# Attention and gated FFN on one core: which head pairs score with unsplit float32 q and k, where the last outputs are staged, and a rewritten order

## The chip, the cores and the metric

One core of one Trainium2 chip runs the whole program in one launch. The metric is device time in microseconds (us). The engines are named as in the profile: PE (TensorE, matmuls), PEld (its weight loads), DVE (VectorE), ACT (ScalarE), POOL (GpSimd) and SP, which here only issues DMAs.

## The reference

```python
# attention: B=8 batches, H=8 heads, S=576, D=64, float32
q_rot, k_rot = rotate(q), rotate(k)          # rotary embedding, halves of 32
scores = matmul(q_rot, k_rot.T) / sqrt(64)
attn = exp(scores - max(scores)); attn /= sum(attn) + 1e-9
x = concat_heads(attn @ v)                   # (8, 576, 512)
# gated FFN
gate = sigmoid(causal depthwise conv of x, 5 taps)
out = (gate * (x @ w_val)) @ w_out           # w_val, w_out: 512 x 512
```

The weights and the conv taps arrive as 64-bit numbers, whose two 32-bit words the kernel turns into float32 itself (`decode`, line 677).

## The kernel before

The 64 heads are worked in 32 pairs (`p`, line 786): the two heads of a pair sit in partitions 0 to 63 and 64 to 127. Four pairs make one batch, whose FFN follows. For one pair the jobs are these:

- **Load and rotate.** q and k arrive (`load`, L300, L304), each with a copy whose halves are swapped. DVE or POOL multiply both by the table (`rope_mul`, L312) and add them (`rope_add`, L318). Pair 0 alone takes another way: its swap and sum are matmuls on PE (`rope_mm`, L327) in plain float32, 288 columns at a time.
- **Split or not.** A pair in `WHOLE` (pairs 4 to 11) keeps its rotated q and k as float32: `rope_add` writes them where the matmul reads them. Every other pair is split: `qk_hi` (L342 to L346, on ACT, DVE or POOL) rounds to the shorter type float32r, and `qk_lo` (L352 for q on DVE, L355 for k on DVE or POOL) writes the remainder.
- **Scores.** There are four blocks of 128 rows of q by 576 columns of k (`s_mm`, L392) and a fifth that both heads share (`s_mix`, L402). A block of one head is two matmuls of 288 columns in an unsplit pair, and six in a split one (high x high, high x low, low x high). A float32 matmul is two records in the trace, a float32r one is one, so an unsplit pair has 32 records on L392 and a split one 48. From pair `APART` = 4 on, one job makes a block for both heads, their matmuls taking turns between the upper and the lower half of PE's rows; pairs 0 to 3 make the block of one head after the other.
- **Softmax.** DVE copies the scores out of PSUM and takes the row maximum (`s_max`, L428), ACT takes the exponential and its sum (`s_exp`, L436): nine of each per pair.
- **Transposes and values.** PE transposes the result (L412), ACT or DVE copy it back (`t_copy`, L505, L507), PE multiplies by v (L518, L528), and DVE scales (L577).
- **Gate and FFN.** Five taps (L603 to L611), a tanh (L616), a split of x (L584 to L591), then for every batch 2 x 4 accumulators of 288-column matmuls (`f_mm`, L636) with split operands. Their results go out through `o_out` (L671 on ACT, L672 on DVE) into one of two staging tiles `outs`, and by `o_dma` (L675) on SP's queue to memory. The last batch makes its accumulators of 256 and 320 columns (L898).

The eight 128-row pieces of the two weight matrices are decoded in nine steps each beside pairs 0 to 5 (`weight_step`: L688 to L690 the first, L703 the rounding).

The order of all of this is written out: `ORDER` (line 37) lists some 3,100 jobs by number, each with the engine that takes it where there is a choice (V is DVE, A is ACT, G is POOL) and with its buffer slots. `Plan.run` issues them just so, and every engine works its own instructions in that order. `FILLS` puts groups of transposes without use on PE at two steps (L443): 20 ahead of pair 0 and 5 before pair 1. PSUM has four slots for score, transpose and FFN tiles alike. `kin` has two buffers, `qin` one.

Of the kernel before, what the change touches and what calls it, by code (L numbers as in the profile page):

```python
# [33 lines left out]
APART = 4  # L34
LIFT = 0
WHOLE = range(4, 12)
ORDER = """
7 24 8 11 17 0:0 35 10 30V 113 12V 31V 13V 32:0 25V 9 14:1 1 26V 33 18V 104 19V 140 36V 15 20:2 2 3 16 27:3 37V 4 21 34 38:1 28 22 5 23A 29 114V 51:0
115 42:2 116 6 45:3 52:00 119G 147 105G 43:11 53 60:0 106 39 48:2 46:2 44 41 142G 40 47 377:100 61:23 54:3 216 49:0 153 141G 57:1 55:1 50 58:32 56
66:0 143V 59 149V 144A 76:2 148V 82A:0 74:3 62 67<149 150V 77A:0 63:1 68:0 145G 151A 72:2 64:1 75A:0 152 292 146A 107 65 223 163:0 117 378A 154:1 218V  # L40
73A 217V 160:3 69 155:02 120G 157:2 161:3 156 78:1 164:11 70 166:3 219G 79A 71 158:0 85:0 80 165 83 172:1 293G 87V:0 167:22 162 88:0 175:2 173:1 86A
294G 159 169:3 176:33 81A 186:1 225V 84A 178:2 110A 89 224V 92:0 174 177 226V 93 194A:1 108 227A 118 90 168 228 91 170:0 299 220G 94 111V 171 179<177
379 187A:1 221V 184:3 229 180:1 121G 488 190:1 185A:1 95 242:2 181 109 131 230:3 243:03 222A 182 191A 195:0 295G 192 183 231:12 188:2 96A:0 197 236:1
189A 300V 248:3 301V 244 239:2 237:0 193A 302G 232 249:1 245:1 296A 240:23 233:3 112G 303A 246:32 251:2 199A:1 304 241 200:1 204:1 238 380 493 234:3
98A:0 202 132G 381 250 205 490V 235 201 382 203 247 252:0 297G 196V 264:3 253 198V 489V 254:2 265A:0 556 260:0 122 133 97V:1 298A 262:3 270A:0 261A
# [24 lines left out]
1010:3 1003:0 791A 1016:0 1009 908V 760:1 761 1208V 904A:3 762 1011<908 1019A:0 1210V 763 1004 1012:2 966:2 1204A 1211V 968 1274V 1002 969 1026V:0  # L70
1013 1205G 1212 1017A:0 967 1344 759 970 1279 1014 1058:30 1052G 1015 1273G 971 764<1211 1059:11 765 792G 766 1061:20 1027:2 767 909V 1029 1062 793:3
1024 768 974A:2 794 795 1346G 1028V 1060 796 1025V 1063:01 975V 1030A 1206A 1031A:0 797<1030 769A 1032:0 1066:3 1022:2 910G 1057 798 1064:2 1023A 799
800 1020:1 1067 801 1033 972G:4 1073:02 1021A 1280G 1084:3 1076:00 1034:1 1085A:1 1281V 1036 1077 1074:31 1282G 1035 976V 1075 1065 1037 802V 1038
770V 1078:2 781G 1039 1068:30 1094A:1 1040A:0 1275G 824:1 1042A:3 1071:3 1079<1094 825 1069:0 803G 1283A 834:0 826 1080:1 1070 835 977V 836 1276A 837
1284 827 1090:3 1277V 1351 1086:2 1091A:1 1043V 838<1277 839 1044G 1087A 840 828<1043 1072 841 1214:32 1081 842V:1 829 973G:3 1215:12 843 830 831 1416
1217:20 1219:03 1213 1082 832A:0 905V:1 804:2 1216 1220:3 1088:1 1353G 1218 805 1083 1222:1 1097:0 806 1089A 807 978V 1092 1223 1095 1229:31 1352G
1098V 1096V 1278A 1221 808<1098 1093V 809 1232:02 911 810 811 1099A:1 1230:30 1224:10 1100:1 812A:1 1345V 1240:3 1227:1 1234:2 1241A:0 1225:3 1242:0
1354V 1101 1286:13 1243A:0 1045V 1235<1354 1231 1104:0 1355V 1233 813 1287:10 1102 1250A:0 1347V 1226 1103 1046V 1228 1356 1105 979 1348V 1423 1288
1106 1236:2 1349G 1246:1 1289:23 1237 1107 1291:23 1417G 1247A 1572 833 1244:0 1292:1 1290 814:1 1238 1041G:0 815 1239 1245A 1294:0 1248:2 1251 816
1418V 1252A 817 1293 1253 1296:30 1110G:1 1255V:0 1295 1256:0 818<1255 1425G 1297:02 1249A 819 820 1108A:1 1299:33 821 1306:3 1254V 1350G 1109V:4  # L80
822A:1 1301:02 1257 1298 1322V:1 1424G 1312:1 1302:1 1307<1322 1313A:1 1304:0 1258:0 1426G 1308:2 1300 1363:21 1111V 1047 1314:3 1427A 1260 1112V 1303
1428 1309 1259 1113V 1305 1579 1261 1366:13 1315A:1 1310 1114G 1262 1364:21 1138:1 1285 1263 1139 1358:32 1264A:2 1419G 1140 1361:2 1316:0 1141 1359:0
1362 1116:2 1574V 1117 1266A:0 1118 1317V 1581G 1119 1420A 1142<1266 1367 1143 1573V 1144 1365 1323:3 1145 1311 1320 1421V 1127:0 1321A 1128 1146 1644
# [146 lines left out]
def attn_gated_ffn(ctx: ExitStack, tc: tile.TileContext, q2, k2, v2, tab, w_val, conv_w, w_out, out, collect=None):  # L230
# [443 lines left out]
    def o_dma(b, oc, lo, hi):  # L674
        SP.dma_start(out=out[b, oc * 128:(oc + 1) * 128, lo:hi], in_=ffn[b, "o", oc, lo])  # L675
# [312 lines left out]
```

## Time and profile before

| | us |
|---|---|
| median of three runs | 632.68 |
| lowest run | 631.52 |
| highest run | 1190.62 |
| the profiled execution's own time | 632.25 |
| its span, first to last instruction | 630.5 |

The profiled execution is 0.43 us under the median, and 1.75 us of it lie outside its span. The mean granted TensorE clock was 0.996 of full speed. In the profile a busy PE is one whose modelled matmuls overlap without a gap; it can be busy and still advance slowly.

### The profile page before, as it was taken

Reading aid. Unit: us, or ns where it says so; the run is one execution under the profiler, and the core shown is the slowest. Engines: PE = TensorE matmul, PEld = TensorE weight load, DVE = VectorE, ACT = ScalarE, POOL = GpSimd, SP = SyncE. Lnnn points to the kernel's source line nnn. Section 1 sums busy time; section 2 is a strip of 40 time slices with the busy share of each in tenths; the row PEclk is TensorE's granted clock in tenths of the full one; section 3 lists DMA queues with packets and bytes.
Section 4 is the critical chain, followed back from the end, with each engine's and each line's share of the span. In section 5 each row is a group of like instructions: output and inputs, shape, how many; then the busy total and the mean of one; then the engine's idle time right before and its main releaser. Section 6 shows DMA issues by size and latency. Waiting matters only on the chain.

```text
span 630.5 us, 21237 instructions
## 1 busy us (share of the span) xinstructions
PE 621.6 (99%) x8782; PEld 523.5 (83%) x8782; DVE 541.3 (86%) x1120; ACT 466.1 (74%) x976; POOL 324.2 (51%) x296
## 2 busy tenths in 40 slices
PE   8999999999999999999999999999999999999997
PEld 7878669777797888969888889788888889889696
DVE  6999999998898898989989899889987889786571
ACT  3999998987777797688788749777787665768502
POOL 2545354454547636656665665663456765640320
PEclk9899999999999999999999999999999999999999
DMA  7546535233543233335343244234243243121102
GB/s 226 182 149 193 163 114 163 82 119 114 154 135 117 91 108 131 99 96 152 117 150 124 61 121 148 90 121 123 93 138 98 80 144 108 59 62 39 60 21 76
DMA packets 42723, 72.85 MB, mean 116 GB/s; under 512 B 15450, under 2 KB 18051, under 8 KB 42627
## 3 DMA queue, kind: packets, MB, share of 16 engines
q1 hardware_dynamic: 42082, 70.91, 36.2%
q8 instruction: 69, 1.13, 0.8%
q10 hardware_dynamic: 544, 0.59, 0.3%
q14 instruction: 28, 0.22, 0.1%
HBM read 61.89 MB, written 9.59 MB: 113 GB/s over the span
## 4 chain that ended last, share of the span: by engine, by line
PE 91%; DVE 4%; ACT 3%; issue 1%; ACTq 0%; POOL 0%; DVEq 0%; POOLq 0%
PE ps_f L636 32%; PE ps_a L518 19%; PE ps_s L392 17%; PE ps_t L412 12%; PE ps_s L402 5%; PE ps_a L528 3%; ACT p L436 2%; DVE p L428 1%; PE ps_f L443 1%; PE ps_s L412 1%; DVE qin L312 1%; ACT pt L505 1%; DVE q L352 0%; PE ps_r L327 0%; ACT o L671 0%
## 5 line engine op out<-in xcount | busy, mean ns | idle before, releaser
L436 ACT ACTIVATE p<-p,nm 128x576 f32<-128x576 f32 x256 | 197.1, 772 | 43.3 <-DVE p L428 43.0
L428 DVE TENSOR_SCALAR_CACHE_REDUCE p<-ps_s 128x576 f32<-128x576 f32 x256 | 185.0, 751 | 32.4 <-PE ps_s L392 24.9
L505 ACT COPY pt<-ps_t 128x1024 f32<-128x1024 f32 (+1 forms) x137 | 128.0, 942 | 43.1 <-PE ps_t L412 41.5
L392 PE MATMUL ps_s<-k,q 64*128 64x288 f32 x1408 | 146.8, 321 | 0.7 <-DVE p L428 0.4
L518 PE MATMUL ps_a<-pt,v 128*64 128x320 f32 (+1 forms) x1024 | 132.1, 409 | 0.2
L392 PEld LDWEIGHTS ps_s<-k,q 64*128 64x128 f32 x1408 | 116.3, 185 | 17.0 <-issue 4.1
L636 PE MATMUL ps_f<-y,wout_hi 64*128 64x288 f32 (+2 forms) x1024 | 111.2, 302 | 0.7 <-ACT o L671 0.6
L518 PEld LDWEIGHTS ps_a<-pt,v 128*64 128x64 f32 x1024 | 70.2, 137 | 48.8 <-issue 2.2
L412 PEld LDWEIGHTS ps_t<-ident,p 64*128 64x128 f32 x2172 | 90.2, 139 | 11.6 <-DVE p L428 2.8
L412 PE MATMUL ps_t<-ident,p 64*128 64x64 f32 x2172 | 96.6, 225 | 0.7 <-ACT pt L505 0.6
L606 DVE SCALAR_TENSOR_TENSOR g<-x,cw,g 128x576 f32<-128x576 f32 (+2 forms) x108 | 92.7, 866 | 1.9 <-POOL g L610 1.4
L636 PEld LDWEIGHTS ps_f<-y,wout_hi 64*128 64x128 f32 x1024 | 85.5, 186 | 2.5 <-ACT o L671 1.2
L636 PE MATMUL ps_f<-xh,wval_hi 64*128 64x288 f32 (+2 forms) x512 | 85.3, 316 | 0.0
L636 PE MATMUL ps_f<-y,wout_lo 64*128 64x288 f32 (+2 forms) x512 | 79.7, 292 | 0.0
L636 PE MATMUL ps_f<-xl,wval_hi 64*128 64x288 f32 (+2 forms) x512 | 79.1, 292 | 0.0
L636 PE MATMUL ps_f<-xh,wval_lo 64*128 64x288 f32 (+2 forms) x512 | 79.1, 292 | 0.0
L312 POOL TENSOR_TENSOR kin<-kin,tab 128x576 f32<-128x576 f32 x38 | 54.0, 1424 | 32.5 <-DVE g L606 19.5
L636 PEld LDWEIGHTS ps_f<-xh,wval_hi 64*128 64x128 f32 x512 | 51.7, 186 | 2.0 <-DVE p L428 1.0
L636 PEld LDWEIGHTS ps_f<-y,wout_lo 64*128 64x128 f32 x512 | 52.5, 185 | 0.0
L636 PEld LDWEIGHTS ps_f<-xl,wval_hi 64*128 64x128 f32 x512 | 51.6, 185 | 0.6 <-POOL xl L591 0.2
L636 PEld LDWEIGHTS ps_f<-xh,wval_lo 64*128 64x128 f32 x512 | 51.5, 184 | 0.0
L436 ACT ACTIVATION_READ_ACCUMULATOR p<-p,nm 128x1 f32 x256 | 48.6, 190 | 0.0
(132 smaller groups left out, 945.6 us busy)
## 6 DMA issues: line engine op xcount, KB each, us to landing
kin<-in_k SPq DMA_DIRECT2D x31, 576.0 KB
qin<-in_q SPq DMA_DIRECT2D x31, 512.0 KB
v<-in_v SPq DMA_DIRECT2D x32, 320.0 KB
out_t<-o SPq DMA_DIRECT2D x28, 288.0 KB
rb<-rd SPq DMA_DIRECT2D x31, 144.0 KB
rb<-rd SPq DMA_DIRECT2D x31, 128.0 KB
wst<-in_w_val SPq DMA_DIRECT2D x4, 512.0 KB
o<-in_w_out SPq DMA_DIRECT2D x4, 512.0 KB
```

The source lines that it names most:

```text
L312: return eng.tensor_tensor(out=t[:, i, a:b], in0=t[:, 0 if p < RAW else i, a:b], in1=table[:, i, a:b], op=ALU.mult)
L392: T.matmul(out=tiles[h][:, half, 0:288], lhsT=operand(p, "q", h, x, c * 128, c * 128 + 128), rhs=operand(p, "k", h, y, k0 + half * 288, k0 ...
L402: inst = T.matmul(out=st["s8"][:, half], lhsT=operand(p, "q", h, x, 512, 640), rhs=operand(p, "k", h, y, D + half * 288, D + half * 288 + ...
L412: T.transpose(out=bank[0:src.shape[1], x, k * D:(k + 1) * D], in_=src[rows], identity=ident[rows, rows])
L428: return V.tensor_scalar(out=to, in0=st[f"s{i}"], scalar1=-SCALE if p in WHOLE else -1.0, scalar2=None, op0=ALU.mult, op1=ALU.min, accum_o ...
L436: return A.activation(out=to, in_=to if lifted else st[f"s{i}"], func=AF.Exp, bias=st[f"nm{i}"], scale=-1.0 if lifted else 1.0, accum_out= ...
L443: T.transpose(out=bank[:, 0, 0:128], in_=ident, identity=ident)
L505: return A.copy(out=dst, in_=src)
L518: T.matmul(out=st[f"a{g}"][HEAD[h], 0:n], lhsT=st["v"][:, j, h, :], rhs=st[f"pt{g}"][:, h * 4 + j], start=(j == 0), stop=False)
L528: T.matmul(out=st[f"a{x}"][HEAD[h], 0:n], lhsT=st["v"][rows, 4, h, :], rhs=st["ptr"][rows, h, 0:n], start=False, stop=True)
L606: return eng.scalar_tensor_tensor(out=g, in0=x_sb, scalar=w, in1=g, op0=ALU.mult, op1=ALU.add)
L636: inst = T.matmul(out=acc[:, x, 0:hi - lo], lhsT=wt[w][HEAD[h], kc, dc * 128:(dc + 1) * 128], rhs=mv[HEAD[h], lo:hi], start=(turn == 0 and ...
```

## The change

- `WHOLE` becomes pairs 0 to 6: seven unsplit pairs in place of eight. Pairs 0 to 3 lose their rounding and remainder steps, pairs 4 to 6 stay as they are, pairs 7 to 11 gain those steps.
- `APART` becomes 1: only pair 0 makes its blocks one head at a time.
- The five transposes without use before pair 1 go.
- In the last batch, six of the eight pieces of output are staged in the halves of `kin0`, `kin1` and `qin0`, which are free by then, and one of their DMAs is issued on ACT's queue.
- `ORDER` is a new list (3,087 jobs in place of 3,096), with other choices of engine.

```diff
-APART = 4
+APART = 1
-WHOLE = range(4, 12)
+WHOLE = range(0, 7)
...
-FILLS = {13: (20, 0), 102: (5, 0)}
+FILLS = {13: (20, 0)}
...
+    def spare(b, oc, lo):
+        i = oc + 4 * (lo > 0) - 2
+        return ("kin0", "kin1", "qin0")[i // 2] + f"#{i % 2}" if b == NB - 1 and i >= 0 else None
+
     def o_out(b, two, oc, lo, hi, eng):
-        o = ffn[b, "o", oc, lo] = outs[:, plan.slots.pop(0), 0:hi - lo]
+        t = spare(b, oc, lo)
+        t = ins[t[0]][int(t[3])][:, int(t[5])] if t else outs[:, plan.slots.pop(0)]
+        o = ffn[b, "o", oc, lo] = t[:, 0:hi - lo]
...
     def o_dma(b, oc, lo, hi):
-        SP.dma_start(out=out[b, oc * 128:(oc + 1) * 128, lo:hi], in_=ffn[b, "o", oc, lo])
+        (A if b == NB - 1 and oc == 3 and lo else SP).dma_start(out=out[b, oc * 128:(oc + 1) * 128, lo:hi], in_=ffn[b, "o", oc, lo])
...
-                        add("VA", o_out, b, two, dc, x, y, r=acc, w=f"oo/{b}.{at}".replace("#", "."))
-                        add("S", o_dma, b, dc, x, y, r=f"oo/{b}.{at}".replace("#", "."))
+                        to = spare(b, dc, x)
+                        to = toks(to + ".@", R3 if to[0] == "q" else R2) if to else f"oo/{b}.{at}".replace("#", ".")
+                        add("VA", o_out, b, two, dc, x, y, r=acc, w=to)
+                        add("S", o_dma, b, dc, x, y, r=to)
```

What this makes of the order is shown at three places. The first is PE from pair 0's scores (L392, L402) to pair 1's, the transposes of pair 0 (L412) between them. Before:

```order
L392 MATMUL ps_s<-k_155,q_147 128x288 x42
L412 MATMUL ps_s<-ident,p 128x64 x4
L402 MATMUL ps_s<-k_155,q_147 128x288 x6
L412 MATMUL ps_t<-ident,p 128x64 x32
L402 MATMUL ps_s<-k_155,q_147 128x288 x6
L392 MATMUL ps_s<-k_155,q_147 128x288 x6
L412 MATMUL ps_t<-ident,p 128x64 x16
L443 MATMUL ps_f<-ident 128x128 x5
L392 MATMUL ps_s<-k_283,q_343 128x288 x24
```

Now:

```order
L392 MATMUL ps_s<-k_156,q_164 128x288 x16
L412 MATMUL ps_t<-ident,p 128x64 x16
L412 MATMUL ps_s<-ident,p 128x64 x4
L402 MATMUL ps_s<-k_156,q_164 128x288 x2
L412 MATMUL ps_t<-ident,p 128x64 x16
L402 MATMUL ps_s<-k_156,q_164 128x288 x2
L412 MATMUL ps_t<-ident,p 128x64 x16
L392 MATMUL ps_s<-k_239,q_296 128x288 x4
L412 MATMUL ps_t<-ident,p 128x64 x16
```

Pair 0's 48 float32r score matmuls on L392 have become 16 float32 ones without a break, and pair 1 starts with one block for both heads, without the five transposes ahead of it.

The second place is ACT over the exponentials of pair 0 (L436) and what stands between them: copies of transposes (L505), the rounding of pair 1's q and k (L346, L363), and steps of the weight decode (`wst`, `l`, `wval_hi`; L688 and L703 before, L694 and L709 now). Before:

```order
L436 ACTIVATE p,sums_85<-p,nm 128x576
L346 ACTIVATE q_147<-ps_r 128x256
L436 ACTIVATE p,sums_85<-p,nm 128x576 x5
L346 ACTIVATE k_283<-kin_70 128x576
L505 COPY pr<-ps_s 128x2x2x64
L436 ACTIVATE p,sums_85<-p,nm 128x576
L505 COPY pt_330<-ps_t 128x2x8x64
L346 ACTIVATE q_343<-qin_71 128x640
L505 COPY pt_364<-ps_t 128x2x8x64
L363 CAST k_283<-k_283 128x2x64
L436 ACTIVATE p,sums_85<-p,nm 128x576
L688 ACTIVATE l<-o 128x512
```

Now:

```order
L694 ACTIVATE wst<-wst 128x512
L436 ACTIVATE p,sums_85<-p,nm 128x576
L709 CAST wval_hi<-wst 128x512
L436 ACTIVATE p,sums_85<-p,nm 128x576 x5
L505 COPY pt_268<-ps_t 128x2x8x64
L436 ACTIVATE p,sums_85<-p,nm 128x576
L505 COPY pt_292<-ps_t 128x2x8x64
L436 ACTIVATE p,sums_85<-p,nm 128x576
L505 COPY pt_292<-ps_t 128x2x8x64
L436 ACTIVATE pm,sums_85<-pm,nm 128x576
```

The two roundings and the cast of pair 1 are gone from ACT, and two steps of the weight decode have come in. Ahead of the first FFN matmul ACT has 5 `qk_hi` jobs in place of 10 and 11 weight steps in place of 7; DVE has no `qk_lo` there in place of 9.

The third place is the end of ACT's list: the results of the last batch (L671 before, L677 now). Before:

```order
L616 ACTIVATE g<-g 128x576
L616 ACTIVATE g<-g 128x256
L661 CAST y_11196<-g 128x256
L671 ACTIVATE o<-ps_f 128x256
L616 ACTIVATE g<-g 128x320
L671 ACTIVATE o<-ps_f 128x256 x3
L671 ACTIVATE o<-ps_f 128x320 x4
```

Now, with the end of DVE's list behind it (L678):

```order
L677 ACTIVATE o<-ps_f 128x576
L616 ACTIVATE g<-g 128x256
L661 CAST y_11265<-g 128x320
L677 ACTIVATE o<-ps_f 128x256
L677 ACTIVATE kin_69<-ps_f 128x256 x2
L681 DMA out_t<-qin_71 128x320
L677 ACTIVATE kin_70<-ps_f 128x320
```

```order
L660 CAST y_11265<-g 128x320
L664 TENSOR_TENSOR y_11276<-g,y_11265 128x320 x2
L678 TENSOR_SCALAR o<-ps_f 128x256
L678 TENSOR_SCALAR qin_71<-ps_f 128x320 x2
L678 TENSOR_SCALAR kin_70<-ps_f 128x320
```

Before, ACT took all eight pieces; now DVE takes four of them, and the last two pieces lie one on each engine.

## Rows read from the trace of the kernel before

**Rows 1.** The page: busy us, share of the span, instructions, by engine.
```profile
PE 621.6 (99%) x8782; PEld 523.5 (83%) x8782; DVE 541.3 (86%) x1120; ACT 466.1 (74%) x976; POOL 324.2 (51%) x296
```

**Rows 2.** The page: the chain that ended last, by engine.
```profile
PE 91%; DVE 4%; ACT 3%; issue 1%; ACTq 0%; POOL 0%; DVEq 0%; POOLq 0%
```

**Rows 3.** Stretches, L392 alone: start:end, length, busy (x instructions) by engine, clock, DMA.
```profile
11.00:68.00 57.00, 26.09 (x194) 22.86 (x194) 0.97 0.56 181
68.00:212.00 144.00, 38.09 (x256) 24.16 (x256) 1.00 0.39 120
212.00:584.00 372.00, 82.61 (x960) 69.24 (x960) 1.00 0.35 109
```

**Rows 4.** The same stretches, L402 alone.
```profile
11.00:68.00 57.00, 5.99 (x48) 4.24 (x48) 0.97 0.56 181
68.00:212.00 144.00, 11.20 (x64) 5.16 (x64) 1.00 0.39 120
212.00:584.00 372.00, 25.78 (x240) 18.67 (x240) 1.00 0.35 109
```

**Rows 5.** First stretch, L443 alone.
```profile
11.00:68.00 57.00, 0.77 (x5) 0.53 (x5) 0.97 0.56 181
```

**Rows 6.** Timeline of PE: start, us, instructions [idle before, releaser].
```profile
8.01 0.65 PE L327 MATMUL ps_r<-kin,swap 128*128 128x288 f32 x2
8.50 0.65 PE L327 MATMUL ps_r<-kin,ident 128*128 128x288 f32 x2
...
17.62 0.48 PE L412 MATMUL ps_s<-ident,p 64*128 64x64 f32 x4 [1.09 <-ACT p L436]
```

**Rows 7.** Stretches of 2 us, all engines; PEclk stands behind the engines.
```profile
16.00:18.00 2.00, 0.91 (x13) 0.68 (x9) 2.00 (x7) 1.30 (x3) 1.18 (x1) 0.86 1.03 407
18.00:20.00 2.00, 2.00 (x32) 1.99 (x32) 1.73 (x5) 2.00 (x7) 0.00 (x0) 0.50 0.88 355
20.00:22.00 2.00, 2.00 (x33) 2.00 (x31) 1.93 (x3) 2.00 (x4) 0.47 (x1) 0.78 0.07 24
```

**Rows 8.** Stretches: DVE alone in two, then PE alone in the second.
```profile
24.00:93.70 69.70, 68.57 (x154) 1.00 0.50 157
93.70:216.00 122.30, 109.10 (x213) 1.00 0.39 116
...
93.70:216.00 122.30, 122.30 (x1670) 1.00 0.39 116
```

**Rows 9.** Stretches, ACT: all of it, then L688 alone.
```profile
24.00:93.70 69.70, 66.35 (x143) 1.00 0.50 157
...
0.00:94.00 94.00, 2.73 (x4) 0.98 0.54 172
```

**Rows 10.** Stretch, L346 alone (ACT).
```profile
0.00:68.00 68.00, 5.31 (x10) 0.97 0.59 190
```

**Rows 11.** Timeline of ACT: first and last of the five L346 of pair 0.
```profile
7.73 0.38 ACT L346 ACTIVATE q<-ps_r 128x256 fp32r<-128x256 f32 x1 [0.93 <-PE ps_r L327]
...
14.10 0.36 ACT L346 ACTIVATE q<-ps_r 128x256 fp32r<-128x256 f32 x1
```

**Rows 12.** Stretches, L352 alone (DVE).
```profile
0.00:68.00 68.00, 3.61 (x6) 0.97 0.59 190
...
212.00:630.00 418.00, 15.56 (x19) 1.00 0.33 102
```

**Rows 13.** Stretches, L355 alone (DVE, then POOL).
```profile
0.00:68.00 68.00, 1.65 (x3) 2.85 (x2) 0.97 0.59 190
...
212.00:630.00 418.00, 7.59 (x9) 14.25 (x10) 1.00 0.33 102
```

**Rows 14.** The chain in order of time: start, us, what.
```profile
48.49 3.04 ACT p L436 x8
```

**Rows 15.** Timeline of the last microseconds: PE, then ACT.
```profile
624.52 0.56 PE L636 MATMUL ps_f<-y,wout_hi 64*128 64x320 f32 x4 [0.58 <-ACT o L671]
...
626.64 0.77 ACT L671 ACTIVATE o<-ps_f 128x320 f32<-128x320 f32 x2 [2.17 <-PE ps_f L636]
```

More of the change, by code (lines that the diff above doesn't have):

```diff
@@ new lines @@
+575A 399 578A:1 572A 611:3 579:1 400 614 631:1 373V 620:02 667A 673V 632A:0 401<667 269V 402 580 612 621:21 403 821G 404 623:32 270 625:1 820V 615:02
+641A:0 405 395A 374G 626<641 384A 618:0 633:3 624 668G 627:3 357:014 581:2 674A 616:2 582 622 675 583 619 334V 826 628 584 335V 617 396V 585 891
+634A:0 336V 677:10 676 586 358A 629 669G 635:3 521A:4 385G 678:01 637:2 636A 680:10 408:1 409 359 638A 682:03 337V 679 410 630 827G 683:3 411 681
+639:2 685:2 642 644 684 828V 692:03 645A 646A:0 829V 643A 412<684 647:0 338 413 693:21 414 640A 822G 415 686 695:30 687:20 406A 416 893G 697:3 823A
@@ new lines @@
+1061 1205:12 1275 1267A 803<1337 1342 1073 1206:02 961G 804 817A:0 805 1208:10 806 1079:1 807V:1 1210:02 1080A 1074 1336G 808 1081:3 1211:1 1083:1
+1082A 1088 1086 1213:3 1268G 779:0 780 1031V 1089A 1090A:1 781 1087A 782 1209 1407 1220:23 1204 1084V 1269A 1027G:1 1214 1091:1 783<1269 1338G 1221:20
+784 1207 785 1223:33 786 1212 1215:12 1343G 787V:1 1233:3 1216:2 1225:0 1344G 1234A:0 1218:1 1231:1 1217 1277:23 1232V:0 1092 1345G 1222 1226<1217
+1095:1 1227:2 1339G 1280:00 818 1093 1228 1346G 1408V 962 1096 1224 1347 1094 1219 1028V:1 1414 1097 1241A:0 1278:12 1229 1237:3 1032G 1230 1098
@@ new lines @@
+1595:20 1166 1640G 1167 1593:31 1168 1605:2 1169V:0 1400G:2 1460 1779 1171:0 1606A:0 1710V 1172 1173 1596 1174 1587:32 1716V 1641A 1462A:1 1581 1463:1
+1175<1462 1459V 1715G 1176 1588:3 1594 1455 1177 1590:0 1456A 1178 1461A 1603:3 1717V 1179A:1 1597:2 1402V 1604A:0 1180 1649:10 1330V 1464 1613A:0
+1609:3 1591 1650:02 1331G 1598<1613 1262 1652:11 1465:1 1718A 1599:0 1466 1589 1780V 1467 1651 1711V 1610A 1403V 1468 1719 1600 1469 1781V 1786
+1654:02 1601 1470 1712G 1611:3 1602 1614 1655:3 1181:1 1170 1616 1182 1404V 1617A 1183 1612A 1473V:4 1151:0 1653 1657:2 1184 1782G 1152 1615A 1474V
@@ new lines @@
+2369 2526G 2409:32 2403:01 2370 2410 2456G 2413:3 2406:0 2419:2 2429A:1 2404:3 2531G 1925:1 2679 2420A:1 2414<2429 2421:0 2415:2 2457A 2223:2 2407
+2224 2533V 1926 2416 2373V:2 1927 2422A:1 1928 2374V 2225 2226 2527V 2412 2470:30 2148V 2405 1929<2527 2471:00 1930 2534A 2417 2227<2405 2680G 2473:12
+2472 1931 1932 2535 2465:30 1933A:0 2228 2681V 1934 2229 2464 2468:1 2230 2375G 2423:1 2392 2466:3 2425:0 2231 2234:3 2426A 2235 2418 2424V 2432:2
+2528G 2236 2474 2237 2430 2427 2078 2480:01 2751 2433V 2371A:4 2220V 2238<2433 2434A:1 2469 2239 2481:20 2435:1 2221G 2240 2686 2467 2483:32 2241
@@ new lines @@
+2895 2276 2757V 2585 2704:32 2833G 2277:3 2705 2586 2764 2713:1 2587A:1 2443G:0 2708:02 2729V:0 2589A:3 2448V 2714<2729 2278 2707 2711:1 2279 2588G:1
+2280 2715:3 2712 2719:2 2709:2 2297:1 2444G:0 2716 2298 2720V:0 2299 2710 2727:0 2300 2717 2723:2 2515G:2 2718 2590V 2281<2709 2724A 2732 2282 2825V
+2283 2284 2516V:3 2730 2301<2590 2285A:1 2734V:0 2725:2 2449G 2731V 2735:0 2591V 2733A 2628:3 2692 2728A 2629 2726A:0 2302 2303 2304 2721:0 2736
+2305V:0 2834G 2617:2 2722A 2630 2592V 2631 2618 2835 2619 2770:10 2593V 2902 2620 2594 2826G 2773:20 2632<2593 2633 2771:31 2634 2286 2635 2896G
@@ L160 @@
+3068 3085V 3069 3084 3070 3086 3071V 3073A 3074 3072
 """
[L161 removed]
+FILLS = {13: (20, 0)}
 class Plan:
```

223 lines of the change are left out of this document (101 added, 122 removed).

## The prediction

> **What bounds the kernel now.** I read the page first: PE is busy for 621.6 us of 630.5 [rows 1], and the chain that ended last lies on PE for 91% of the span [rows 2]. So what the change does to PE's own work is the first thing to price. Next I read stretches. From 93.7 us, where the first FFN matmul starts, to 216 us PE is busy without a gap, and DVE for 109.10 of 122.30 us [rows 8]: there PE alone is the bound. Between 24 and 93.7 us, where there is no FFN work yet, DVE is busy for 68.57 of 69.70 us [rows 8] and ACT for 66.35 [rows 9]. Three engines are full together there, and the chain in order of time goes through ACT, as in eight exponentials' records in a row at 48.49 us [rows 14]. Less work on PE is therefore worth its whole price after 93.7 us, and before that only as far as DVE and ACT get faster too. The last view is the end, where PE waits once more for an output piece and ACT takes the last two one after the other [rows 15].
>
> **The change part by part.** The sum is made against the profiled execution, 632.25 us, which is 0.43 us under the median.
>
> *A pair's scores on PE.* Pairs 0 to 3 (split, one head at a time) take 26.09 us on L392 [rows 3] and 5.99 on L402 [rows 4], together 32.08, or 8.02 us a pair. The eight unsplit pairs take 38.09 + 11.20 = 49.29, or 6.16. The twenty split pairs with both heads at a time take 82.61 + 25.78 = 108.39, or 5.42. Neighbours overlap in these numbers, so I use their differences alone.
>
> - Pairs 1 to 3 go from 8.02 to 6.16: 3 x 1.86 = **5.6 us less**.
> - Pairs 7 to 11 go from 6.16 to 5.42: 5 x 0.74 = **3.7 us less**.
> - Pair 0 becomes unsplit but stays one head at a time, which no row shows. The nearest is pair 0's rotation: float32 matmuls of 288 columns that no second row half accompanies, two records each, start 0.49 us apart (8.01 to 8.50) [rows 6]. Eight blocks of one head with two such matmuls make 7.84, and the fifth block 11.20 / 8 = 1.40, so 9.24: **1.2 us more**. If its price were that of the unsplit pairs that take turns, it would be 1.9 less; I take 1.2 more, since its row has the same type, width and lack of a partner.
> - The five transposes without use go: 0.77 us [rows 5], taken as **0.8 less**; the gap that they filled may be idle instead, so the other end is nothing.
>
> *The cover ahead of the first FFN matmul.* There PE loses 5.6 - 1.2 + 0.8 = 5.2 us. DVE loses nine remainders, 3.61 us on L352 [rows 12] and 1.65 on L355 [rows 13], 5.26 together: it keeps step. ACT doesn't. Of its ten roundings, 5.31 us [rows 10], the five of pair 0 stay as plain copies (0.38 for the first, 0.36 for the last [rows 11], so about 1.85), which frees 3.5. The new order puts four more steps of the weight decode on it ahead of that point (the order's second place): 2.73 us for four of them [rows 9]. About 0.8 us is left. The rest can only come out of ACT's idle time in that stretch, 69.70 - 66.35 = 3.35 us. So the early gain lies between 0.8 us (ACT idles as now) and 0.8 + 3.35 = 4.2 (it never idles). I take 3.2, nearer the upper end, because ACT waits there for PE and DVE and both have 5 us less to do. That gives back **2.0 us** of the 5.2.
>
> *Pairs 7 to 11 off PE.* They gain ten remainders, at 15.56 / 19 = 0.82 us for q on DVE [rows 12] and 7.59 / 9 = 0.84 for k on DVE, or 14.25 / 10 = 1.43 on POOL [rows 13]. All ten on DVE are 8.3 us; DVE is idle for 122.30 - 109.10 = 13.2 us in the stretch that holds most of them [rows 8], so I cost them at nothing. If that cover were gone, the pairs would gain nothing: the 3.7 are then the price. The roundings fall to ACT, which is less busy there than DVE.
>
> *What the number of passes would say.* The rows have the unsplit pairs 14% over the split ones (6.16 to 5.42). The Trainium skill, FP8 and Floating Point Precision, TensorE Precision Notes, says that true float32 takes four passes through the array. Against three float32r matmuls that would be 4 to 3; by it an unsplit pair would be 7.23 us, pairs 1 to 3 would give only 2.4 and pairs 7 to 11 would give 9.0. The trace disagrees with that ratio, and it decides.
>
> *The end.* PE's last wait for an output piece is 0.58 us [rows 15]. Eight tiles instead of two leave no reason for it but PSUM, so I take it as gone. The last two pieces, 0.77 us in a row on ACT [rows 15], lie on ACT and DVE at once, which is half of that, 0.38. One more DMA issue now stands ahead of the last one on SP's queue, so I count 0.3 for the pair: **0.9 us less**, between 0.2 and 1.3. ACT's issue of one DMA stands ahead of its last piece; it waits for a piece that DVE has made before, so I cost it at nothing, and it is inside that range.
>
> *The sum.* -5.6 - 3.7 + 1.2 - 0.8 + 2.0 - 0.9 = -7.8 us, and 632.25 - 7.8 = 624.45: I forecast **624.5 us**, 1.3% under the median. With every term at its bad end (0.8 early, nothing from pairs 7 to 11, 0.2 at the end) it is 631.25; with the early gain at 4.2 and the end at 1.3 it is 632.25 - 9.2 = 623.05.
>
> **The rivals.**
>
> - *The clock stays at full (0.11).* PE idles for 1.09 us at 17.62, waiting for pair 0's exponentials [rows 6], and its granted clock is 0.86, 0.50 and 0.78 in the three stretches around it [rows 7], the lower level of 1.2 GHz for part of them. Full would be 2.4; the three lose 0.28 + 1.00 + 0.44 = 1.7 us. Pair 0's sixteen float32 matmuls now run for about as long as DVE takes to empty them, so the idle and the slow stretch could both go: 2.8 us, and with nothing given back to ACT the sum is -9.8 - 2.8 = -12.6, so **619.7**. Against it: two waits of pair 0 on ACT's exponentials are left in the order, and pair 1's q is still multiplied on DVE behind eight maxima.
> - *ACT and DVE keep the old pace early and in the middle (0.15).* All terms at their bad ends: **631.3**. For it: ACT is 95% busy already, and POOL's weight steps moved to it.
> - *The lengthened q chain holds PE in pairs 7 to 11 (0.08).* Slower than before. `qin` has one buffer; a split pair adds a rounding and a remainder (0.82 us on DVE [rows 12], about as much on ACT) between the sum and the first score matmul, and these pairs also keep `qin` longer, so the next load comes later. PE takes the FFN's jobs in a fixed order and can't step past a late block. At 1.6 us a pair, the two steps alone, the gain is gone (5 x 1.6 = 8.0); with a late load on top, 2.4 us a pair, 12 - 7.8 = 4.2 us are lost: **636.5**. It decides from 1.6 us a pair. Against it: DVE's 13.2 us of idle time, and the twenty split pairs behind, which have the same chain.
> - *The price is by passes (0.05).* If unsplit pairs really cost PE a third more than split ones and the rows hide it in the overlap, pairs 1 to 3 give 2.4, pair 0 costs 8.02 / 3 = 2.7 and pairs 7 to 11 give 9.0: with 0.8 and 0.9 that is -10.4, **621.9**, nearly all of it behind 117 us and nothing to give back early. By the Trainium skill's passes this is the case; by the rows it is not.
>
> **How the numbers follow.** My own case has 0.61. The range from 618.5 to 633.0 holds that case with both ends of its bounds (623.05 to 631.25), the clock's 619.7, the passes' 621.9 and the old pace's 631.3, and leaves the late q chain and part of each other case outside, about 0.18. A difference of 2% (below 620.0 or above 645.3) is about what a measurement of this kernel can tell from no change. Faster than that is the clock's case and little else: 0.11. Slower needs the late chain at twice its price: 0.03. The same has 0.86.
>
> **What would show it.** In the changed profile L392 and L402 take about 6.2 us in each of pairs 1 to 3, 9.2 in pair 0, and 5.4 in pairs 7 to 11. The first FFN matmul starts near 90.5 us instead of 93.7, with ACT busy for over 97% of the time before it. From there to 216 us PE has no gap, and DVE is above 90%. The end has no wait of PE for an output piece. I am wrong if PE waits for q or k in pairs 7 to 11, if the first FFN matmul starts later than 93 us, or if pair 0 alone eats what pairs 1 to 3 give.

## The result and the profile after

The changed kernel takes **624.13 us** (median of 4 runs, 623.81 to 624.25), the kernel before 632.17 beside it on the same chip (one of its four runs, of 1190.62, is left out of the ratio). The ratio is 0.9875, with a 95% interval from 0.9856 to 0.9895: 1.25% faster, which by 2% counts as the same. The forecast was 624.5. The profiled execution took 624.21 us, with a span of 622.4 against 630.5.

The page of the changed kernel, the busy row and the chain's shares by engine, beside [rows 1, 2]:

```profile
PE 613.2 (99%) x8797; PEld 515.0 (83%) x8797; DVE 539.1 (87%) x1122; ACT 465.9 (75%) x983; POOL 319.1 (51%) x293
...
PE 89%; DVE 4%; ACT 2%; issue 2%; DMA 1%; POOL 0%; SPq 0%; DVEq 0%; POOLq 0%
```

By shares these rows hardly tell the kernels apart; PE's busy time fell by 8.4 us, about what the span lost. Where that went is told by the start of the same matmul in both timelines of PE:

| first matmul of | before | after | difference | predicted |
|---|---|---|---|---|
| pair 0's scores | 11.1 | 10.3 | -0.8 | |
| pair 1's scores | 23.4 | 20.4 | -3.0 | |
| pair 4's scores | 68.0 | 60.5 | -7.5 | |
| the FFN | 93.7 | 88.5 | -5.2 | -3.2 |
| pair 12's scores | 216.2 | 207.1 | -9.1 | -6.9 |
| end of the span | 630.5 | 622.4 | -8.1 | -7.8 |

So 5.2 us were gained ahead of the first FFN matmul, 3.9 from there to pair 12's scores, and 1.0 was given back behind them. Two of these starts don't bound the same work. Ahead of the first FFN matmul PE has the same transposes and value matmuls in both orders. But between pair 4's first scores and that matmul the new order has 80 records of value matmuls (L518) where the old one has 64, and 128 of transposes (L412) where the old one has 144. It has moved pair 4's scores ahead of other work, so part of the -7.5 is no gain. And in the stretch with pairs 7 to 11 the new order has 16 transposes and 6 FFN records fewer, first before, then after (records, busy us, mean ns, idle before):

```profile
L412 PE MATMUL ps_t<-ident,p 64*128 64x64 f32 x440 | 18.9, 223 | 0.0
L636 PE MATMUL ps_f<-y,wout_hi 64*128 64x288 f32 x180 | 20.2, 313 | 0.0
L636 PE MATMUL ps_f<-y,wout_lo 64*128 64x288 f32 x90 | 13.5, 292 | 0.0
```

```profile
L412 PE MATMUL ps_t<-ident,p 64*128 64x64 f32 x424 | 18.3, 222 | 0.0
L636 PE MATMUL ps_f<-y,wout_hi 64*128 64x288 f32 x176 | 18.8, 299 | 0.2 <-DVE qin L318 0.2
L636 PE MATMUL ps_f<-y,wout_lo 64*128 64x288 f32 x88 | 14.4, 292 | 0.0
```

These 22 records stand behind pair 12's first scores now. They take about 1.0 us: 0.6 by the two rows of L412, and 0.4 by the starts of six such FFN records in the kernel before (215.45 to 215.84). That is the 1.0 given back. For the same work, then, 5.2 us were gained ahead of the first FFN matmul, 2.9 in the stretch with pairs 7 to 11, and nothing at the end.

Ahead of the first FFN matmul, stretches of the kernel before, in the columns of [rows 7] (start:end, length, then busy time of PE, PEld, DVE, ACT, POOL, clock, DMA): up to 24 us, and the whole.

```profile
10.30:24.00 13.70, 12.06 (x126) 10.74 (x126) 13.29 (x34) 10.34 (x26) 5.46 (x5) 0.88 0.60 212
...
10.30:93.70 83.40, 80.89 (x947) 62.63 (x945) 81.86 (x187) 76.69 (x167) 40.27 (x38) 0.98 0.52 166
```

The same stretches after, and the one from 24 us on:

```profile
10.30:24.00 13.70, 12.51 (x127) 10.01 (x126) 12.74 (x35) 12.54 (x27) 7.16 (x6) 1.00 0.84 275
24.00:88.50 64.50, 63.23 (x735) 42.24 (x733) 63.15 (x142) 62.94 (x142) 33.15 (x28) 1.00 0.51 157
10.30:88.50 78.20, 75.73 (x859) 52.26 (x859) 75.89 (x176) 75.48 (x167) 40.31 (x34) 1.00 0.57 177
```

The stretch is 5.20 us shorter. DVE's work in it fell by 5.97 (81.86 to 75.89), ACT's by only 1.21, while ACT's idle time fell by 3.99 (from 83.40 - 76.69 = 6.71 to 78.20 - 75.48 = 2.72). Of DVE's 5.97, 4.40 are remainders that are gone (3.24 on L352 and 1.16 on L355 in this stretch); the rest comes with the new order, whose choices of engine among other things give five of DVE's sixteen rotation multiplies (L312) to POOL. PE, DVE and ACT are now each busy for 97% of the stretch. Of ACT's 3.99, 2.20 lie before 24 us (3.36 to 1.16), in a part that the prediction's window had left out.

The three stretches of [rows 7] are at full clock now:

```profile
16.00:18.00 2.00, 1.39 (x26) 1.15 (x26) 2.00 (x7) 2.00 (x6) 1.41 (x1) 1.00 0.73 272
18.00:20.00 2.00, 1.53 (x28) 1.01 (x26) 2.00 (x4) 2.00 (x6) 0.00 (x0) 1.00 0.80 214
20.00:22.00 2.00, 2.00 (x35) 1.84 (x33) 1.19 (x4) 2.00 (x4) 1.78 (x2) 1.00 0.60 164
```

PE still idles there, for 0.61 and 0.47 us in two waits in place of one of 1.09 [rows 6], but the granted clock stays at 2.4 GHz. L392 of pair 0, of pairs 1 to 3 and of pairs 4 to 6 (PE, PEld, clock, DMA), beside [rows 3]:

```profile
10.20:16.30 6.10, 5.92 (x32) 4.40 (x32) 1.00 0.98 337
20.40:60.00 39.60, 16.53 (x96) 10.06 (x96) 1.00 0.58 175
60.40:112.00 51.60, 14.48 (x96) 9.66 (x96) 1.00 0.39 120
```

Pair 0, one head at a time, takes 5.92 where 7.84 was predicted. Pairs 1 to 3 take 5.51 a pair and pairs 4 to 6 take 4.83, although both run the same 32 records a pair with turns: the number is not a price that goes with the form. The other score line, L402, of pair 0 and of pairs 1 to 3:

```profile
10.20:20.30 10.10, 1.46 (x8) 0.61 (x8) 1.00 0.90 301
20.40:60.00 39.60, 4.29 (x24) 1.83 (x24) 1.00 0.58 175
```

The end, beside [rows 15] (start, us, engine, tile, idle before and its releaser):

```profile
618.09 0.49 DVE L678 TENSOR_SCALAR kin<-ps_f 128x320 f32<-128x320 f32 x1 [0.87 <-PE ps_f L636]
618.62 0.44 ACT L677 ACTIVATE kin<-ps_f 128x320 f32<-128x320 f32 x1 [4.27 <-DVE kin L678]
```

The last two pieces lie on two engines, but still one after the other: ACT's is released by DVE's. From PE's last matmul to the end of the span it is 4.35 us, against 3.95 before.

### The profile page after: what moved, and what is told of

Read it like the earlier page. It is cut to its first block, busy times and chain, and to the rows that moved or that the text cites. A ratio compares the mean times of both kernels' runs of the same rounds, so it can differ in the third digit from the quotient of the medians.

```text
span 622.4 us, 21260 instructions
## 1 busy us (share of the span) xinstructions
PE 613.2 (99%) x8797; PEld 515.0 (83%) x8797; DVE 539.1 (87%) x1122; ACT 465.9 (75%) x983; POOL 319.1 (51%) x293
## 4 chain that ended last, share of the span: by engine, by line
PE 89%; DVE 4%; ACT 2%; issue 2%; DMA 1%; POOL 0%; SPq 0%; DVEq 0%; POOLq 0%
PE ps_f L636 32%; PE ps_a L518 20%; PE ps_s L392 17%; PE ps_t L412 11%; PE ps_s L402 4%; PE ps_a L528 3%; DVE p L428 2%; ACT pt L505 1%; DMA qin<-in_q 1%; ACT p L436 1%; PE ps_f L443 1%; PE ps_s L412 1%; PE ps_r L327 1%; DVE qin L312 0%; DVE pm L428 0%
## 5 line engine op out<-in xcount | busy, mean ns | idle before, releaser
L436 ACT ACTIVATE p<-p,nm 128x576 f32<-128x576 f32 x256 | 196.9, 771 | 25.8 <-DVE p L428 25.3
L505 ACT COPY pt<-ps_t 128x1024 f32<-128x1024 f32 (+1 forms) x136 | 124.0, 921 | 45.2 <-PE ps_t L412 43.9
L392 PE MATMUL ps_s<-k,q 64*128 64x288 f32 x1424 | 140.5, 319 | 0.7 <-ACT pr L505 0.4
L518 PE MATMUL ps_a<-pt,v 128*64 128x320 f32 (+1 forms) x1024 | 133.0, 410 | 0.2
L392 PEld LDWEIGHTS ps_s<-k,q 64*128 64x128 f32 x1424 | 110.7, 185 | 19.1 <-issue 5.9
L518 PEld LDWEIGHTS ps_a<-pt,v 128*64 128x64 f32 x1024 | 69.9, 137 | 49.5 <-issue 2.5
L636 PE MATMUL ps_f<-y,wout_hi 64*128 64x288 f32 (+2 forms) x1024 | 109.5, 300 | 0.2 <-DVE qin L318 0.2
L412 PEld LDWEIGHTS ps_t<-ident,p 64*128 64x128 f32 x2172 | 89.6, 139 | 8.6 <-issue 2.3
L412 PE MATMUL ps_t<-ident,p 64*128 64x64 f32 x2172 | 95.4, 223 | 1.1 <-ACT pr L505 0.7
L606 DVE SCALAR_TENSOR_TENSOR g<-x,cw,g 128x576 f32<-128x576 f32 (+2 forms) x105 | 88.2, 852 | 0.7 <-ACT g L608 0.2
L312 POOL TENSOR_TENSOR qin<-qin,tab 128x640 f32<-128x640 f32 x29 | 45.2, 1561 | 35.7 <-DVE g L606 13.5
L312 POOL TENSOR_TENSOR kin<-kin,tab 128x576 f32<-128x576 f32 x30 | 42.5, 1422 | 30.3 <-DMA kin<-in_k 11.9
L636 PEld LDWEIGHTS ps_f<-xh,wval_hi 64*128 64x128 f32 x512 | 53.0, 186 | 2.5 <-issue 1.1
L636 PEld LDWEIGHTS ps_f<-xl,wval_hi 64*128 64x128 f32 x512 | 52.9, 185 | 0.1
L636 PEld LDWEIGHTS ps_f<-xh,wval_lo 64*128 64x128 f32 x512 | 52.8, 185 | 0.0
```

The source lines that it names most:

```text
L312: return eng.tensor_tensor(out=t[:, i, a:b], in0=t[:, 0 if p < RAW else i, a:b], in1=table[:, i, a:b], op=ALU.mult)
L392: T.matmul(out=tiles[h][:, half, 0:288], lhsT=operand(p, "q", h, x, c * 128, c * 128 + 128), rhs=operand(p, "k", h, y, k0 + half * 288, k0 ...
L412: T.transpose(out=bank[0:src.shape[1], x, k * D:(k + 1) * D], in_=src[rows], identity=ident[rows, rows])
L436: return A.activation(out=to, in_=to if lifted else st[f"s{i}"], func=AF.Exp, bias=st[f"nm{i}"], scale=-1.0 if lifted else 1.0, accum_out= ...
L505: return A.copy(out=dst, in_=src)
L518: T.matmul(out=st[f"a{g}"][HEAD[h], 0:n], lhsT=st["v"][:, j, h, :], rhs=st[f"pt{g}"][:, h * 4 + j], start=(j == 0), stop=False)
```

## The experiments

The theory in the first four runs was the prediction's: PE's work on the scores sets the pace, wholly behind the first FFN matmul and in part ahead of it. The rival for the early stretch was that DVE and ACT set it there, whatever PE's blocks look like.

**Pairs 7 to 11 undone.** The changed kernel with these pairs unsplit again. The rounding and remainder steps leave the order; the sums write q and k themselves, at the place where the rounding stood.

```diff
-WHOLE = range(0, 7)
+WHOLE = range(0, 12)
```

> The changed kernel, but pairs 7 to 11 unsplit again: their twenty rounding and remainder steps go, each rotated sum is written at the place of the rounding step. Theory (a score block on PE costs what the stretches say, and PE alone is the bound after 93.7 us): 5 x 0.74 us come back, 627.8 us against 624.1. Rival (elementwise work counts, PE's form of score does not): twenty steps fewer, so no slower than 624.1, perhaps 1 to 2 us faster.

It takes 629.14 us, ratio 0.9955 [0.9939, 0.9971]: 5.0 us more than the changed kernel, nearly all of it from pairs 7 to 11 (the first FFN matmul starts 0.3 us later, pair 12's scores 5.2). L392 of the five pairs, there L391, then in the changed kernel:

```profile
110.00:212.00 102.00, 24.78 (x160) 15.80 (x160) 1.00 0.38 117
```

```profile
110.00:207.00 97.00, 21.29 (x240) 17.61 (x241) 1.00 0.40 121
```

That is 3.5 us on this line, and 1.0 on the other score line (7.51 to 6.51). A wait of PE has also come in, in the list of waits (total, times, longest):

```profile
PE ps_f L635 <- POOL k L317: 1.0, 1, 1.0
```

So the term for pairs 7 to 11 is right in its cause, and here 5.0 where 3.7 was expected. The wait is no price of a score block: it stands right behind a sum of k on POOL, which starts at 102.94 here and at 100.53 in the changed kernel. Without it 4.0 are left.

**Pairs 1 to 3, one head at a time again.**

```diff
-APART = 1
+APART = 4
```

> The changed kernel, but pairs 1 to 3 make their unsplit blocks one head after the other, as before the change. Theory: a block then costs twice pair 0's 0.70 us a head, 1.40, against 1.07 to 1.13 with turns, so 12 blocks x 0.3 = 3.6 us, 627.7. By the price the prediction used for pair 0 (0.98 a head) it would be 12 x 0.85 = 10 us, 634. Rival (the early stretch is held by ACT and DVE, PE's form doesn't matter there): 624 to 625.

It takes 624.33 us, ratio 0.9879 [0.9861, 0.9897]: no difference from 624.13. The step of the prediction that priced the turns falls. The first FFN matmul starts at 89.6 instead of 88.5, and the 1.1 us shrink to 0.7 by the end.

**Pairs 1 to 3, split again, with turns.** The rounding goes on ACT and the remainder on DVE (q) and POOL (k), right behind each sum. The second line of the edit gives pairs 1 to 3 tiles of their own for q and k.

```diff
-WHOLE = range(0, 7)
+WHOLE = (0, 4, 5, 6)
...
-        key = (n, p % 2, p in WHOLE, p < WHOLE[0])
+        key = (n, p % 2, p in WHOLE, p > 3)
```

> The changed kernel, but pairs 1 to 3 split again, with turns between the heads; the rounding (on ACT) and the remainder (q on DVE, k on POOL) stand right behind the sum. PE's own score work falls by 3 x 0.74 = 2.2 us. Theory (three engines are full together ahead of the first FFN matmul): ACT gets about 4.2 us and DVE 2.5 us more, so it is slower, 626 to 629. Rival (PE's sum alone decides): 622.

It takes 634.53 us, ratio 1.0041 [1.003, 1.0053]: 10.4 us more, far beyond what the theory expected. The first FFN matmul starts at 99.5. PE now waits, in the list of waits:

```profile
PE ps_s L412 <- ACT p L436: 2.5, 2, 1.9
PE ps_t L412 <- DVE pm L545: 2.1, 1, 2.1
```

Its granted clock also falls to the lower level twice, in these stretches (all engines):

```profile
23.00:27.00 4.00, 3.78 (x39) 3.34 (x41) 3.59 (x9) 3.27 (x7) 3.03 (x3) 0.57 0.65 216
47.00:54.00 7.00, 5.78 (x32) 3.69 (x31) 6.03 (x14) 6.36 (x15) 3.21 (x3) 0.51 0.62 216
```

The 10.4 hold this, and the price of places in the order that nobody has tuned, so they show that these steps can hold up PE, not what they must cost.

**The unsplit form alone, in the old order.** The kernel before with pairs 0 to 3 unsplit, one head at a time as before.

```diff
-WHOLE = range(4, 12)
+WHOLE = range(0, 12)
```

> The kernel before, its order and its one-head blocks, but pairs 0 to 3 unsplit too (pairs 0 to 11): only their rounding and remainder steps go. Theory: PE's blocks get little cheaper (1.40 against 1.54 us a block by the trace, 16 blocks, 2.2 us), and DVE and ACT are freed of 5 and 3.5 us in the stretch where all three are full: 2 to 4 us faster than before, 628 to 630. Rival (the new order is the gain): 631.5 to 632.5, no change.

It takes 639.2 us, ratio 1.0117 [1.0099, 1.0135]: slower, against the expectation. One row of PE and two stretches (all engines) show where:

```profile
27.15 0.74 PE L443 MATMUL ps_f<-ident 128*128 128x128 f32 x5 [2.19 <-DVE pm L545]
```

```profile
24.00:30.00 6.00, 3.81 (x27) 2.50 (x27) 3.40 (x10) 2.61 (x6) 4.24 (x4) 0.86 0.25 86
30.00:36.00 6.00, 6.00 (x38) 4.39 (x35) 2.44 (x8) 4.91 (x12) 0.00 (x0) 0.58 0.01 3
```

The five transposes without use stand in front of PE's list and wait 2.19 us for DVE; all they need besides a PSUM slot is an identity matrix that has been there since the start, so it is the slot that they wait for. Afterwards PE counts as busy without a gap, but its granted clock is 0.58, the lower level of 1.2 GHz for most of that stretch.

**The same without the five transposes.**

```diff
-FILLS = {13: (20, 0), 102: (5, 0)}
+FILLS = {13: (20, 0)}
```

> The kernel that lost (the order of before, pairs 0 to 11 unsplit, pairs 0 to 3 one head at a time), now without the five transposes without use ahead of pair 1. In its trace they wait 2.19 us for a PSUM slot that DVE empties, at 27 us, and a stretch at half clock follows (granted clock 0.58 from 30 to 36 us). If these five are the cause of the loss, most of the 7.2 us come back: 632 to 634. If the loss is the order's (the scores of pair 1 queue behind a slot that DVE empties in any case), PE waits as long for the score block behind them: 637 to 640.

It takes 633.15 us, ratio 1.0015 [1.0003, 1.0027]: 6.05 us come back. Yet the kernel is no faster than before, though the nine remainders on DVE and the roundings of pairs 1 to 3 on ACT are gone: the first FFN matmul starts at 93.9, against 93.7.

**The kernel before without the five transposes.** The same edit in the kernel before, nothing else.

> The kernel before without the five transposes without use, nothing else. My prediction: 0.8 us less (631.3), or nothing if the gap that they filled stays idle. Rival, from the kernel whose order of before and unsplit pairs lost: there the five cost 639.2 - 633.15 = 6.05 us, because they waited for a PSUM slot; if that holds in the kernel before too, several us less (628 or lower). In its trace they did not wait, so I expect 631 to 632.5.

It takes 632.08 us, ratio 1.0016 [0.9997, 1.0036]: no difference. PE's row where they stood (the profiled execution took 638.49):

```profile
23.12 3.62 PE L392 MATMUL ps_s<-k,q 64*128 64x288 f32 x22 [1.02 <-ACT k L363]
```

With split pairs they fill a gap, in which PE waits for pair 1's k anyway; my 0.8 us less is not there.

**The same settings in the new order.** The changed kernel with pairs 0 to 11 unsplit and pairs 0 to 3 one head at a time, so that PE has the same matmuls as in the kernel of 633.15.

```diff
-APART = 1
+APART = 4
...
-WHOLE = range(0, 7)
+WHOLE = range(0, 12)
```

> The changed kernel's order with the settings of the kernel that lost (pairs 0 to 11 unsplit, pairs 0 to 3 one head at a time). Theory (behind the first FFN matmul PE's scores alone set the pace, ahead of it they don't): 624.1 + 5.0 + 0.2 = 629.3 us, and the 9.9 us to 639.2 are the order's alone. Rival (the one-head blocks cost PE their price once nothing else is gained): 629.1 + 3.6 = 632.7. Rival (the form, not the order, made that kernel lose): 637 or more.

It takes 629.07 us, ratio 0.9948 [0.993, 0.9965], as the theory expected. The new order, with its choices of engine and the new staging at the end, is worth 633.15 - 629.07 = 4.1 us. (The staging by itself is worth nothing, see below.) The gain lies early, in the stretch up to the first FFN matmul, first in the old order, then in the new one:

```profile
10.30:93.90 83.60, 81.44 (x862) 56.97 (x860) 78.86 (x177) 73.65 (x160) 36.60 (x35) 1.00 0.52 167
```

```profile
10.30:89.00 78.70, 75.48 (x860) 53.83 (x858) 75.71 (x174) 75.11 (x167) 40.39 (x34) 1.00 0.55 175
```

This pair of rows is worth the most. The same matmuls, at full clock in both, make PE busy for 81.44 us in one order and for 75.48 in the other. In the old order ACT is idle for 9.95 us and DVE for 4.74: no engine is short of time, and each waits in turn for another. In the new one all three are at 95% or more. Work has also changed engines: DVE has 3.15 us less, ACT 1.46 more and POOL 3.79 more. The rotation multiplies, L312 (DVE, POOL), in the old order and in the new one:

```profile
10.30:93.90 83.60, 12.43 (x16) 11.34 (x8) 1.00 0.52 167
```

```profile
10.30:89.00 78.70, 8.98 (x11) 18.68 (x13) 1.00 0.55 175
```

No run has the old engines in the new sequence, or the new engines in the old one, so which of the two gives the 4.1 us is not shown.

**Score matmuls by themselves.** 24 blocks for both heads in each of four forms, back to back on PE. Of the kernel everything else is left out; ahead of the blocks stand only the loads, copies that make q and k, and 60 transposes without use.

```python
for n in range(24):
    for hs in ((0, 1),) if turns_ else ((0,), (1,)):
        for half in range(2):
            for t, (x, y) in enumerate(tt):   # one term unsplit, three split
                for h in hs:
                    T.matmul(...)
```

> Leaves out everything but score matmuls: PE alone runs 24 blocks for both heads in each of four forms, back to back, in the order unsplit with turns, unsplit one head at a time, split with turns, split one head at a time. By the rows of the two kernels a block for both heads costs 38.09/8/4 = 1.19 us unsplit with turns (24 of them 28.6 us), 82.61/20/4 = 1.03 split with turns (24.8 us), 26.09/4/4 = 1.63 split one head at a time (39.1 us). For unsplit one head at a time my prediction's price is 8 x 0.98 / 4 = 1.96 (47.0 us); the changed kernel's pair 0 gives 5.92/4 = 1.48 (35.5 us). If matmuls of the two heads overlap only where they take turns, it is 47; if the end of one head's block overlaps the start of the other's, about 35.

PE alone, the four forms in the order unsplit with turns, unsplit one head at a time, split with turns, split one head at a time (records on an edge count on both sides):

```profile
9.93:33.31 23.38, 23.38 (x192) 1.00 0.01 1
33.31:56.46 23.15, 23.15 (x195) 1.00 0.00 1
56.46:75.77 19.31, 19.31 (x292) 1.00 0.01 3
75.77:95.20 19.43, 19.43 (x292) 1.00 0.01 2
```

An unsplit block takes 23.38 / 24 = 0.97 us and a split one 19.31 / 24 = 0.80, and turns make no difference to either. The 1.63 us of a split block in pairs 0 to 3 [rows 3], twice as long, was not PE's price.

**Pair 0 with turns too.**

```diff
-APART = 1
+APART = 0
```

> The changed kernel with pair 0's scores made for both heads with turns too. By my prediction's prices (9.24 us one head at a time, 6.16 with turns) 3.1 us less, 621.0. By the kernel of score matmuls alone (23.38 us with turns, 23.15 one head at a time, for 24 blocks) and by the changed kernel's own pair 0 (5.92 for L392) there is nothing to gain: 623.6 to 624.6, or a little slower, since the first maxima then start after two heads' blocks instead of one.

It takes 624.22 us, ratio 0.9877 [0.9865, 0.989]: no difference, as the kernel of score matmuls says, and not the 3.1 us of my prices.

**Pairs 4 to 6 split too.** The steps stand right behind each sum, as in the run with pairs 1 to 3 split.

```diff
-WHOLE = range(0, 7)
+WHOLE = range(0, 4)
```

> The changed kernel with pairs 4 to 6 split too (rounding on ACT, remainder of q on DVE, of k on POOL). Theory (ahead of the first FFN matmul DVE and ACT and the chain from q to the scores set the pace): pair 6's scores lie behind it and give 0.7 us; pairs 4 and 5 lie ahead of it and cost up to 10.4/3 = 3.5 us each, so 624 to 630, and the first FFN matmul starts later than 88.5. Rival (PE's price counts everywhere): 3 x 0.74 = 2.2 less, 621.9.

It takes 632.33 us, ratio 1.0003 [0.999, 1.0017], 8.2 us more than the changed kernel and above the range I expected. Two rows, ACT and PE, show one place:

```profile
53.98 0.68 ACT L346 ACTIVATE k<-kin 128x576 fp32r<-128x576 f32 x1 [1.30 <-POOL kin L318]
...
57.91 0.71 PE L412 MATMUL ps_t<-ident,p 64*128 64x64 f32 x16 [3.38 <-ACT pr L505]
```

The rounding waits on ACT for POOL's sum, and what is queued behind it on ACT comes late; PE then waits 3.38 us for a copy of ACT's, and from 58 to 62 us its granted clock is 0.58:

```profile
58.00:62.00 4.00, 3.89 (x34) 2.88 (x36) 2.72 (x7) 3.35 (x7) 2.51 (x3) 0.58 0.62 163
```

**Only pair 6 split too.** Its steps stand a few jobs behind the sums, its remainders both on DVE, and the loads that follow come after them.

```diff
-WHOLE = range(0, 7)
+WHOLE = range(0, 6)
```

> The changed kernel with pair 6 split too, its rounding on ACT and both remainders on DVE. Pair 6's scores start at 96.4 us, behind the first FFN matmul at 88.5; its rounding and remainder fall around that point. Theory (behind it PE's score work alone counts): 0.7 us less, 623.4. Rival (the chain from q and k to the scores holds here as for pairs 4 and 5, whose splitting with pair 6 cost 8.2 us): 8.2/3 = 2.7 more, 626.8. Between them: the steps that fall before 88.5 cost 1.6 us or so of ACT and DVE, 625.

It takes 624.42 us, ratio 0.9874 [0.986, 0.9889]: no difference, between the theory's 623.4 and 625. It does not tell them apart. With the run before it, it says that most of the 8.2 us goes with pairs 4 and 5 or with where the steps stand.

**The new staging of the last outputs alone.** The kernel before with `spare`, `o_out` and `o_dma` of the changed one, the engines of the pieces as before.

> The kernel before with the new staging of the last batch's outputs alone, the order and the engines of its pieces as before. My prediction gave the end 0.9 us in all, of which 0.58 for the wait of PE for an output piece is this part: 631.5. The trace of the changed kernel says that the end after PE's last matmul is not shorter (4.35 us to 3.95): then no difference, 632.0 to 632.2.

It takes 632.13 us, ratio 1.0003 [0.9994, 1.0011]: no difference. PE's wait for an output piece stays, in its list of waits:

```profile
PE ps_f L636 <- ACT qin L677: 1.0, 1, 1.0
```

With a staging tile of its own for the piece, the wait is still there: what PE waits for is ACT, which has not emptied the accumulator. It is longer than before (1.0 against 0.6), with ACT's issue of one DMA (0.35 us) between its two pieces. In the changed kernel, where DVE takes half of the pieces, it is gone; no run has that alone.

None of these kernels beats the changed one.

## Why the prediction was right, and where it was not

The time was right to 0.4 us, and that is luck in part. By stretches the prediction had -3.2 us ahead of the first FFN matmul, -3.7 for pairs 7 to 11 and -0.9 at the end; for the same work it was -5.2, -2.9 and nothing. Too little in the first and too much in the other two cancelled. One of the six terms was right in cause and near in size, that of pairs 7 to 11.

- **Pairs 7 to 11 off PE (-3.7): right.** The trace shows -3.9 between the first FFN matmul and pair 12, of which 1.0 is work moved out of the stretch, so -2.9; the run that undid it 5.0, or 4.0 without the wait that came in. The kernel of score matmuls gives the price by itself: a pair has five blocks (40 records unsplit and 60 split on L392 and L402, 8 and 12 a block), and 5 x (23.38 - 19.31) / 24 = 0.85 us a pair, 4.2 for the five, against my 0.74 and 3.7 from the rows. The size thus lies between 2.9 and 4.2.
- **Pairs 1 to 3 on PE (-5.6): wrong in cause.** The step that failed is the subtraction 8.02 - 6.16, which took busy time on L392 in a stretch where three engines wait for each other for the price of the form. One head at a time costs nothing (the runs with APART = 4 and of score matmuls by themselves). By the price of the blocks an unsplit pair costs PE 0.85 us more, so the change gives PE 2.5 us more to do in pairs 1 to 3, where I had it do 5.6 less.
- **The cover ahead of the first FFN matmul (+2.0): wrong in sign of its use.** I let DVE and ACT give back part of a gain of PE's. By the rows they are where the gain lies: DVE's 5.97 us of work less and ACT's 3.99 us of idle time. The net came to -5.2 where I had -3.2 and an upper bound of 4.2. The bound failed because its window began at 24 us and left out 2.20 us of ACT's idle time before it. It takes the shorter work and the new order together: the form in the old order gave nothing (633.15), the new order with the unsplit form 4.1 us (629.07). The new order with the split pairs back, their steps in places not made for them, gave nothing either (634.53).
- **Pair 0 (+1.2): wrong.** Its two score lines take 5.92 + 1.46 = 7.38 us instead of 9.24, and with turns it is no faster: as in the kernel of score matmuls, the two heads' blocks overlap without them. Its nearest row was the rotation's matmuls; they fill all 128 rows of PE, and the scores only 64.
- **The five transposes (-0.8): nothing**, the end I had named and not taken.
- **The end (-0.9): nothing.** PE's wait of 0.58 us went, as predicted, but the way from PE's last matmul to the end is 0.40 longer. The last two pieces are not "at once": 0.49 us on DVE and then 0.44 on ACT.

Of the rivals, the clock's mechanism came true: pair 0's stretch at half clock is gone. Its price did not follow: the kernel of 633.15 is at full clock too and starts the FFN at 93.9. The runs of the kernel before, beside all these experiments, show what the clock is worth there: of 55, 20 had a mean granted clock of 1.000 and a median of 631.5 us, and 27 had 0.994 to 0.997 (the profiled one has 0.996) and 632.3. That is 0.8 us, where I had 1.7 for the slow stretch; and the 1.1 us of idle time beside it has stayed (0.61 + 0.47). ACT and DVE did not keep the old pace. The lengthened q chain in pairs 7 to 11, my first sign of being wrong, came with 0.2 us and no more. From the first FFN matmul to 210 us the changed kernel's list of waits has a single one of PE, for a sum of q:

```profile
PE ps_f L636 <- DVE qin L318: 0.2, 1, 0.2
```

The price by passes is refused by the kernel of score matmuls too: unsplit to split is 23.38 to 19.31, a ratio of 1.21. The Trainium skill, FP8 and Floating Point Precision, TensorE Precision Notes, has four passes for true float32; against three float32r matmuls that makes an estimate of 1.33. The measurement lies between that and the 1.14 of my rows.

Of the signs, ACT is busy for 62.94 of 64.50 us, 97.6%, from 24 us to the first FFN matmul, and DVE for 95% from there to 210 us, both as predicted:

```profile
88.50:210.00 121.50, 115.69 (x227) 1.00 0.39 117
```

That matmul starts at 88.5, earlier than the 90.5 I named. Pairs 7 to 11 take (21.29 + 6.51) / 5 = 5.56 us each on the two score lines, near the 5.4 predicted; pairs 1 to 3 take (16.53 + 4.29) / 3 = 6.94, not 6.2.

What stays open: which of the order's moves, of sequence or of engine, are worth the 4.1 us; what the rounding and remainder steps of pairs 1 to 6 would cost in places made for them; and why undoing pairs 7 to 11 costs 1.1 us more than they gave, beyond the wait of 1.0.

## What to carry to other kernels

Busy time of matmuls is a price only where PE waits for nobody: take it from a stretch in which the other engines have time to spare, or run the matmuls by themselves. Where three engines are full together, count each one's work and idle time over the whole stretch, and ask what the order lets them use. When the starts of two orders are compared, count the work that stands between them first. A change of form and the order that fits it belong together: here the form gained nothing ahead of the FFN without the new order, and the new order, as far as it was tried, nothing without the form.

## What was not expected of the hardware

- Blocks of the upper and of the lower 64 rows of PE overlap as well when six matmuls of one half stand ahead of six of the other (19.43 us) as when they alternate (19.31). Unsplit, 96 matmuls take 23.38 us, 0.24 each, half of the 0.49 of the rotation's matmuls of the same width, which fill all rows [rows 6]. The Trainium skill, TensorEngine Tiling (Array Packing), Key Properties, says that different tiles can run matmuls in parallel; the trace agrees, and shows that taking turns is not needed for it.
- PE's share of busy time hid 6 us of slack in 84 (81.44 against 75.48 for the same matmuls). The Trainium skill, Perfetto Trace Analysis, Identifying the Most-Contended Engine, warns that a matmul's busy share is no good measure of how close a kernel is to its limit; the trace agrees.
- Five transposes worth 0.77 us [rows 5] cost 6.05 us where they had to wait 2.19 us for a PSUM slot, and nothing where they did not. That wait of PE was followed by a stretch at the lower clock (0.58), as was the one of 3.38 us with pairs 4 to 6 split.
